# Chunked attention and a routed mixture of experts on one core: ranking candidates for a table of three slots, and new places for the picking, the evictions and the splits

## The chip, the cores and the metric

The kernel runs on one core of a Trainium2 chip. The metric is the device time of one execution in microseconds; before the change it is 582.98 us, the median of three runs (580.61 to 583.99).

## The reference

Attention runs inside chunks of 64 tokens (8 batches, 8 heads, 576 tokens, head size 64). Its output is the input of a layer of 8 experts, of which each token takes the one with the largest logit.

```python
scores = scale * np.matmul(q_c, k_c.transpose(0, 1, 2, 4, 3))
scores = scores - np.max(scores, axis=-1, keepdims=True)
attn = np.exp(scores)
attn = attn / (np.sum(attn, axis=-1, keepdims=True) + 1e-09)
out = np.matmul(attn, v_c)
...
logits = x @ w_gate + modality_bias[modality_id]
e_idx = np.argmax(logits, axis=1)
...
for e in range(E):
    mask = e_idx == e
    h = np.maximum(x[mask] @ w1[e], 0.0)
    out[mask] = gate_w[mask, None] * (h @ w2[e])
```

x has 4608 rows of 512 values, the hidden size is 1024, and gate_w is the softmax probability of the chosen expert.

## The kernel before

**Attention in rounds.** A round r works on two blocks of 128 tokens. `scores(r)` makes 64 small matmuls into the PSUM tile `sb`, then DVE takes the row maximum (`mx`, L236) and the difference to it (`ex`, L237). `exps` takes the exponent on ACT and adds halves on POOL (`sr`, L245). `transposes` turns `ex` into the two banks `ts`, ACT copies them to `at`; `values` multiplies with v into the same two banks; `evict` copies them to `xt` on ACT (L281). `rows(t)` multiplies a block with the identity and the gate weights at once (L290), into one of the two bank pairs `pairs`; DVE scales the result (`xr`, L292) for the copy `xd` in DRAM, and `parts` copies the gate part to `lp` on ACT (L300). Rounds 0 to 7 run alone, in the loop at L947; the other ten are merged into the first slots by `merge`, one piece at each `tick`. Each engine takes its instructions in the order in which the program emits them (`manual_schedule`), so the order of the calls is the order of the queues.

**Choosing slots.** Tokens are sorted by expert into slots of 384 rows (11 of them, then two of 256). Slot 0 is picked from the first 8 blocks (`route0`): POOL makes the logits (`logits`), DVE finds each token's expert (`gmx` to `oh`, L342 to L347), PE ranks tokens by matmuls with a triangle and with ones (L350, L352), DVE picks the fullest expert and makes a list of rows (`top` to `vm`, L354 to L377), eight small matmuls add it up (L382), and `tk` holds it (L385). `gather` then fetches the rows from `xd` with three indirect DMAs of POOL (L685). Slots 1 to 3 come from a table made after 16 blocks by `early_table`: three times it finds the expert with the most rows left, takes up to 384 of them and subtracts. The other slots come from `slot_table`. `route(g)` ranks the groups of blocks behind the first; it needs a spare bank for its two matmuls (L458, L459), and a running sum over the blocks, `scan`, which DVE makes before them. `blank` and `locate` read rows of the tables into registers of SP, which holds up SP's later DMAs, the fetches of weights among them.

**Experts in steps.** A slot has eight steps f, numbered over all slots g = 8 s + f. `first` makes 12 matmuls (L800) with a tick in their middle, ACT and DVE make `hh` and `hl` of the result; `second` of the step before makes 9 for three tiles (L816). Numbers are split into a high and a low part. For weights this is `wsplit`: a cast `wh` on ACT (L759) and a difference `wl` on DVE (L763), from `raw`, which `fetch` loads two steps at a time. In slot 0, `LEAD` says which splits follow which step; later it is step g + 4, with six buffers. For the rows of slots 0 and 1 PE transposes `xg` (`split`, L726); for later slots it goes by way of DRAM (`stash`, `place`, `turn`, `part`).

**What sets the order.** `PLAN` names, for a round and one of three places in it, calls that are made there. `PREP` does so for the ends of steps. Jobs such as `route` and `early_table` are generators: each `advance` (twice or three times a step, and at each `hook` of a round) runs one piece, up to its next yield.

Of the kernel before, what the change touches and what calls it, by code (L numbers as in the profile page):

```python
# [87 lines left out]
C_END = C_TH3 + NTT + 1  # L88
# [3 lines left out]
def attention_moe(ctx: ExitStack, tc: tile.TileContext, qkv, mod, cst, bias, wcat, wfst, void, out):  # L92
# [60 lines left out]
    th3 = cs[:, C_TH3:C_TH3 + NTT + 1]  # L153

# [71 lines left out]
    def scores(r, bank):  # L226
        b = qks.pop(r)
        sp = bank.rearrange("p u (h k) -> p u h k", h=H)
        for h in range(H):
            for u in range(2):  # L230
                us = slice(u * 64, u * 64 + 64)
                for c in range(2):
                    PE.matmul(sp[c * 64:c * 64 + 64, u, h, :], b[us, 0, h, c], b[us, 1, h, c], start=True, stop=True)  # L233
        ex = exs[r] = ak.tile([P, H, 2, 64], F32, name="ex", bufs=2)
# [94 lines left out]

    def route0():  # L330
# [37 lines left out]
        yield  # L368
# [9 lines left out]
                        val.unsqueeze(2).to_broadcast([P, n, NTT, 2]), ALU.mult)  # L378
        yield
# [25 lines left out]
    def route(g):  # L405
# [7 lines left out]
        early, last = g < NLEV, g == len(GROUPS) - 1  # L413
        l0 = lps[g % 2][:, 0:n]
# [28 lines left out]
        while d < n:  # L443
# [14 lines left out]
        PE.matmul(rp[:, 0, 0:n], ub, oh, start=True, stop=True)  # L458
        PE.matmul(rp[:, 1, 0:n + 1], ones, scan[i][:, off:off + n + 1], start=True, stop=True)  # L459
        V.tensor_tensor(base[g + 1], base[g], rp[:, 1, n], ALU.add)  # L460
        ra = tl("ra")
        V.tensor_tensor(ra, rp[:, 0, 0:n], base[g].unsqueeze(1).to_broadcast([P, n, E]), ALU.add)
# [329 lines left out]
    def first(x, w, f, n):  # L792
# [4 lines left out]
        for k in range(NK):  # L797
# [4 lines left out]
            if k == 1:  # L802
                tick()
# [271 lines left out]
```

## Time and profile before

| | before |
|---|---|
| median of three runs | 582.98 us |
| the profiled execution | 583.71 us |
| its span | 581.9 us |
| PE busy | 532.6 us (92%) |
| DVE busy | 359.9 us (62%) |
| ACT busy | 242.2 us (42%) |
| POOL busy | 165.6 us (28%) |
| mean granted clock of PE | 0.971 |
| HBM read and written | 101.91 MB, 27.83 MB |

Times within the profile are counted from the start of the span. A busy PE says little by itself: where the whole span is 92% busy, the idle 8% and the stretches of low clock are the parts to look at, and a table by windows shows where they lie. In a row of the timeline the brackets hold the idle time of the engine before it and what ended it. Rounds 0 to 7 take the first 66 us, the merged rounds reach to about 200 us, and the steps of the later slots fill the rest.

### The profile page before, as it was taken

The numbers are of one execution on the slowest core, as the hardware profiler recorded it, in microseconds if no ns is written. First come the engines' busy times: TensorE is split into PE (matmuls) and PEld (weight loads), VectorE is DVE, ScalarE is ACT, GpSimd is POOL, SyncE is SP. The second block draws the span as 40 slices with busy tenths as digits, with TensorE's granted clock in tenths as the row PEclk, the third lists the DMA queues.
The fourth block names the chain that finished last, engine by engine and source line by source line (L and its number), as shares of the span: only waits on it lengthen the run. The fifth ranks groups of instructions, "written<-read, shape, count | busy, mean of one in ns | idle before, by whom it ended". The sixth has DMA issues, their size and how long they took to land.

```text
span 581.9 us, 12230 instructions
## 1 busy us (share of the span) xinstructions
PE 532.6 (92%) x4930; PEld 476.1 (82%) x4931; DVE 359.9 (62%) x613; ACT 242.2 (42%) x401; POOL 165.6 (28%) x185
## 2 busy tenths in 40 slices
PE   6886587799878999999999999999999999999993
PEld 3776477688767988898899989889989898998982
DVE  4568557867577596865646556564655656456741
ACT  3444424354535433343434444434343434335530
POOL 3331426523343576042050212204041220402001
PEclk9899978899989999999999999999999999999997
DMA  8999954488758426958596574748667673756400
GB/s 339 402 325 315 355 214 151 149 304 294 271 190 283 150 64 203 336 206 310 175 288 220 161 275 151 274 155 304 202 207 229 170 257 128 244 180 210 175 34 26
DMA packets 48626, 129.83 MB, mean 223 GB/s; under 512 B 7100, under 2 KB 23852, under 8 KB 39600
## 3 DMA queue, kind: packets, MB, share of 16 engines
q1 hardware_dynamic: 36592, 100.35, 51.1%
q0 software_dynamic: 7072, 19.18, 9.2%
q10 hardware_dynamic: 4896, 9.44, 4.4%
q8 instruction: 40, 0.66, 0.5%
q14 instruction: 26, 0.21, 0.1%
HBM read 101.91 MB, written 27.83 MB: 223 GB/s over the span
## 4 chain that ended last, share of the span: by engine, by line
PE 66%; issue 14%; DVE 8%; DMA 7%; POOL 2%; ACT 1%; SPq 0%; POOLq 0%; ACTq 0%; DVEq 0%
PE y L800 24%; PE sb L816 17%; PE t L816 9%; PE t L800 4%; PE y L290 3%; DMA xg<-xd,tk 3%; DMA qk<-in_qkv 2%; PE y L273 2%; DVE wl L763 2%; PE y L233 2%; PE y L258 2%; DVE mx L236 1%; DVE ex L237 1%; PE sb L233 1%; POOL out L831 1%
## 5 line engine op out<-in xcount | busy, mean ns | idle before, releaser
L763 DVE TENSOR_TENSOR wl<-raw,wh 128x1024 fp32r<-128x1024 f32 x104 | 127.2, 1225 | 38.3 <-ACT wh L759 38.2
L800 PE MATMUL y<-xh,wh 128*128 128x384 f32 (+1 forms) x368 | 120.5, 328 | 0.0
L800 PE MATMUL y<-xl,wh 128*128 128x384 f32 (+1 forms) x368 | 120.4, 327 | 0.0
L800 PE MATMUL y<-xh,wl 128*128 128x384 f32 (+1 forms) x368 | 120.0, 326 | 0.0
L806 ACT ACTIVATE hh<-y 128x384 fp32r<-128x384 f32 (+1 forms) x92 | 43.6, 474 | 182.8 <-PE y L800 182.6
L807 DVE SCALAR_TENSOR_TENSOR hl<-y,hh 128x384 fp32r<-128x384 f32 (+1 forms) x92 | 49.1, 534 | 105.6 <-ACT hh L806 105.5
L759 ACT CAST wh<-raw 128x1024 fp32r<-128x1024 f32 x104 | 108.2, 1043 | 6.3 <-DMA raw<-in_wcat 6.1
L831 POOL DMA_INDIRECT out<-yo,tk x37 | 38.0, 1027 | 239.8 <-DVE yo L830 210.7
L816 PE MATMUL sb<-wh,hl 128*128 128x512 f32 x208 | 83.3, 400 | 1.3 <-DVE hl L807 1.3
L816 PE MATMUL sb<-wh,hh 128*128 128x512 f32 x208 | 83.3, 400 | 0.0
L816 PE MATMUL sb<-wl,hh 128*128 128x512 f32 x208 | 82.5, 397 | 0.0
L800 PEld LDWEIGHTS y<-xh,wh 128*128 128x128 f32 x368 | 69.1, 188 | 3.6
L800 PEld LDWEIGHTS y<-xl,wh 128*128 128x128 f32 x368 | 69.2, 188 | 3.4
L800 PEld LDWEIGHTS y<-xh,wl 128*128 128x128 f32 x368 | 69.2, 188 | 0.0
L816 PEld LDWEIGHTS sb<-wh,hl 128*128 128x128 f32 x208 | 39.3, 189 | 11.1 <-DVE hl L807 1.7
L685 POOL DMA_INDIRECT xg<-xd,tk x37 | 42.8, 1156 | 16.6 <-issue 10.7
L480 POOL DMA_INDIRECT tab<-tg,pi x36 | 38.8, 1078 | 23.0 <-issue 12.2
L816 PEld LDWEIGHTS sb<-wh,hh 128*128 128x128 f32 x208 | 39.2, 188 | 5.9
L816 PEld LDWEIGHTS sb<-wl,hh 128*128 128x128 f32 x208 | 39.2, 189 | 5.6
L245 POOL TENSOR_TENSOR sr<-ex 128x512 f32<-128x512 f32 x18 | 24.3, 1351 | 67.9 <-ACT ex L243 67.9
L290 PE MATMUL y<-cs,xt 128*128 128x144 f32 x288 | 41.5, 293 | 1.7 <-DVE e_tab L364 1.3
L290 PEld LDWEIGHTS y<-cs,xt 128*128 128x128 f32 x288 | 38.6, 194 | 3.2 <-DVE base L361 1.4
(225 smaller groups left out, 714.9 us busy)
## 6 DMA issues: line engine op xcount, KB each, us to landing
raw<-in_wcat SPq DMA_DIRECT2D x44, 1024.0 KB, 6.2
qk<-in_qkv SPq DMA_DIRECT2D x18, 1024.0 KB, 7.5
v<-in_qkv SPq DMA_DIRECT2D x18, 512.0 KB, 4.7
xd<-xr ACTq DMA_DIRECT2D x18, 512.0 KB, 7.3
raw<-in_wfst SPq DMA_DIRECT2D x8, 1024.0 KB, 9.5
xs<-xg SPq DMA_DIRECT2D x9, 768.0 KB, 7.7
xq<-xs SPq DMA_DIRECT2D x36, 192.0 KB, 3.8
xs<-xg SPq DMA_DIRECT2D x2, 512.0 KB, 6.6
```

The source lines that it names most:

```text
L233: PE.matmul(sp[c * 64:c * 64 + 64, u, h, :], b[us, 0, h, c], b[us, 1, h, c], start=True, stop=True)
L245: G.tensor_tensor(sring[r % 2][:, :, :, 0:32], exu[:, :, :, 0:32], exu[:, :, :, 32:64], ALU.add)
L290: PE.matmul(fp[:, p, 0:GWC], xt[:, p, :], gw[:, p, :], start=True, stop=True)
L480: w = G.indirect_dma_start(tab, bass.IndirectOffsetOnAxis(ap=pi[:, j:j + 1], axis=0), tg[:, j, :], None, bounds_check=E * CAP - 1, oob_is_ ...
L685: G.indirect_dma_start(xg[:, t, :], None, xd[0:n, :], bass.IndirectOffsetOnAxis(ap=tk[:, t:t + 1], axis=0), bounds_check=n - 1, oob_is_err ...
L759: A.copy(hi, raw)
L763: (G if pool else V).tensor_tensor(lo, raw, hi.bitcast(F32), ALU.subtract)
L800: PE.matmul(hp, a[:, ks], b[:, k, 0:n], start=(m == 0), stop=(m == 3 * NK - 1))
L806: A.activation(hh[:, 0:n], hp, AF.Relu)
L807: V.scalar_tensor_tensor(hl[:, 0:n], hp, 0.0, hh.bitcast(F32)[:, 0:n], ALU.max, ALU.subtract)
L816: PE.matmul(y, a[:, tsl], b[:, DM:2 * DM], start=(f == 0 and i == 0), stop=(f == NF - 1 and i == 2))
L831: w = G.indirect_dma_start(out, bass.IndirectOffsetOnAxis(ap=tk[:, t:t + 1], axis=0), yo, None, bounds_check=N - 1, oob_is_err=False)
```

## The change

- `early_table` no longer takes one maximum after the other. Each expert gives three candidates (its rows left, less 0, 384 and 768), 24 in all. All pairs are compared in one operation (576 results in bf16), a sum over them gives each candidate's rank, and the three with ranks 0, 1 and 2 are selected together with their expert, row and quantity.
- `scores` keeps its matmuls only; `differences` holds mx and ex. In a round the hook stands between the two, and a second one behind them: the picking of slot 0 is emitted there one round earlier, with both of its DVE parts in one piece. Gather, fetch and split calls of `PLAN` move with it.
- `evict(r)` is emitted behind the second `rows` of its own round, ahead of `parts`, with four buffers for `xt`.
- For group 1 the ranking is made by nine matmuls as in `route0`, without the scan. For groups 2 and 3 one more yield stands before the ranking.
- `AHEAD = 3`: weights are split three steps ahead, with five buffers, and slot 0 has at most one split after each of its steps 0 to 2.
- The two splits of slot 1's rows are made inside `first` of steps 6 and 7 (`AMID`); blank, locate, gather and settle of `PREP` move up by a step.

```diff
-    5: {2: ["fetch 0"]},
-    6: {1: ["gather 0"]},
+    5: {3: ["fetch 0"]},
+    6: {0: ["gather 0"], 3: ["hi 0"]},
...
-LEAD = ((2,), (3, 4), (5,), (6,), (7, 8), (9,), (10,), (11,))
+AHEAD = 3
+AMID = {6: "split 1 0", 7: "split 1 2"}
...
-    0: {2: ["choose"], 3: ["blank 1"], 4: ["settle", "locate 1"],
-        5: ["gather 1", "head"], 6: ["locate 2", "locate 3", "split 1 0"], 7: ["split 1 2", "gather 2"]},
+    0: {2: ["choose", "blank 1"], 3: ["settle", "locate 1"],
+        4: ["gather 1", "head"], 5: ["locate 2", "locate 3"], 7: ["gather 2"]},
...
+    def differences(r, bank):
+        sp = bank.rearrange("p u (h k) -> p u h k", h=H)
         ex = exs[r] = ak.tile([P, H, 2, 64], F32, name="ex", bufs=2)
...
+    def rank_tiles(rp, oh, n):
+        PE.matmul(rp, ub, oh, start=True, stop=False)
+        for t in range(n):
+            PE.matmul(rp[:, t + 1:], ones, oh[:, t:t + 1].to_broadcast([P, n - t, E]), start=False, stop=(t == n - 1))
...
         V.tensor_tensor(col, col, rank, ALU.add)
-        yield
         ge = wk.tile([P, n, NTT + 1], F32, name="ge0", bufs=1)
...
-        while d < n:
+        while d < n and not early:
...
+        if not early:
+            yield
         yield "rp"
...
+        V.scalar_tensor_tensor(cand, be(left), 32.0, offs, ALU.mult, ALU.add)
+        cand = cand.rearrange("p e j -> p (e j)")
+        more = t3("more", [C, C], BF16)
+        V.tensor_tensor(more, cand.unsqueeze(1).to_broadcast([P, C, C]), cand.unsqueeze(2).to_broadcast([P, C, C]), ALU.is_gt)
+        yield
+        rank = t3("rank3", [C])
+        V.reduce_sum(rank, more, axis=AX.X)
+        yield
...
+        V.tensor_tensor(ohs, rank.unsqueeze(1).to_broadcast([P, ne, C]), sid[:, 0:ne].unsqueeze(2).to_broadcast([P, ne, C]), ALU.is_equal)
+        sel = t3("sel", [3, ne, C])
...
+        V.reduce_sum(rf, sel, axis=AX.X)
+        yield
...
-    WB = 6
+    WB = 5
...
             if k == 1:
                 tick()
+                if g in AMID:
+                    call(AMID[g])
...
-            if s == 0:
-                for k in LEAD[f]:
+            if s == 0 and f < 4:
+                for k in ((2,), (3,), (4,), (5, 6))[f]:
                     wsplit(k)
-            elif g + 4 < end:
-                wsplit(g + 4)
+            elif g + AHEAD < end:
+                wsplit(g + AHEAD)
...
     for r in range(NPURE):
-        if r:
-            evict(r - 1)
         scores(r + 1, sb)
         hook(r, 0)
+        differences(r + 1, sb)
+        hook(r, 1)
         transposes(r, ts)
         if r:
             rows(2 * r - 2, pairs[0])
         exps(r + 1)
         values(r, ts)
-        hook(r, 1)
+        hook(r, 2)
         if r:
             rows(2 * r - 1, pairs[1])
+        evict(r)
+        if r:
             parts(r - 1)
             put(r - 1)
+        hook(r, 3)
         sums(r)
-        hook(r, 2)
```

How this moves instructions is shown at three places. On DVE, in rounds 5 and 6, the list of slot 0 (`ge` to `vm`, then `idf` and `tk`) stood in two parts; `mx` and `ex` are the maximum and difference of round 6's scores. Before:

```order
L249 TENSOR_REDUCE sm<-sr_145 128x16
L250 RECIPROCAL ris<-sm 128x16
L370 TENSOR_TENSOR ge_912<-col,cs 128x32
L372 SCALAR_TENSOR_TENSOR col<-ge_912,col 128x8
L373 SCALAR_TENSOR_TENSOR col<-ge_912,col 128x8
L374 TENSOR_TENSOR ge_912<-ge_912 128x8x3
L375 TENSOR_TENSOR xg<-xq,col 128x1024
L377 TENSOR_TENSOR vm<-ge_912,val 128x48
L236 TENSOR_REDUCE mx<-sb 128x16
L237 TENSOR_TENSOR ex<-sb,mx 128x2x8x64
L384 TENSOR_SCALAR idf<-y_99 128x3
L385 TENSOR_TENSOR tk_170<-idf,y_99 128x3
```

The same part of DVE's order now (line numbers of the changed kernel):

```order
L382 TENSOR_TENSOR ge_846<-col,cs 128x32
L384 SCALAR_TENSOR_TENSOR col<-ge_846,col 128x8
L385 SCALAR_TENSOR_TENSOR col<-ge_846,col 128x8
L386 TENSOR_TENSOR ge_846<-ge_846 128x8x3
L387 TENSOR_TENSOR xg<-xq,col 128x1024
L389 TENSOR_TENSOR vm<-ge_846,val 128x48
L302 TENSOR_TENSOR xr<-y_98,ris 128x4x4x32
L302 TENSOR_TENSOR xr<-y_99,ris 128x4x4x32
L397 TENSOR_SCALAR idf<-y_99 128x3
L398 TENSOR_TENSOR tk_169<-idf,y_99 128x3
L259 TENSOR_REDUCE sm<-sr_145 128x16
L260 RECIPROCAL ris<-sm 128x16
```

The list is now made ahead of round 5's two xr, and `tk` stands ahead of the next mx and ex. On POOL, the gather of slot 0 (`xg<-xd`) stood behind two `sr` that follow the last logits; before:

```order
L320 TENSOR_TENSOR lg_148<-lg_148,mb 128x16
L245 TENSOR_TENSOR sr_144<-ex 128x16x32
L245 TENSOR_TENSOR sr_145<-ex 128x16x32
L685 DMA xg<-xd,tk_170 128x512 x3
L245 TENSOR_TENSOR sr_144<-ex 128x16x32
```

And now:

```order
L330 TENSOR_TENSOR lg_148<-lg_148,mb 128x16
L255 TENSOR_TENSOR sr_144<-ex 128x16x32
L717 DMA xg<-xd,tk_169 128x512 x3
L255 TENSOR_TENSOR sr_145<-ex 128x16x32
L255 TENSOR_TENSOR sr_144<-ex 128x16x32
```

The gather has one `sr` less ahead of it. On PE, at the end of step 6 and the start of step 7 of slot 0, the split of slot 1's rows (`xg`) stood between the `rows` (`xt`) of two blocks and the next `first` (`t<-xh`, `t<-xl`); `y<-cs,ex` are transposes of attention. Before:

```order
L290 MATMUL y_98<-cs,xt 128x144 x4
L290 MATMUL y_99<-cs,xt 128x144 x4
L726 MATMUL y_98<-cs,xg 128x128 x6
L800 MATMUL t_102<-xh_165,wh_155 128x384
L800 MATMUL t_102<-xl_166,wh_155 128x384
L800 MATMUL t_102<-xh_165,wl_156 128x384
...
L258 MATMUL y_99<-cs,ex 128x128 x8
```

And now:

```order
L300 MATMUL y_99<-cs,xt 128x144 x4
L300 MATMUL y_98<-cs,xt 128x144 x4
L833 MATMUL t_102<-xh_164,wh_158 128x384
L833 MATMUL t_102<-xl_165,wh_158 128x384
L833 MATMUL t_102<-xh_164,wl_159 128x384
...
L268 MATMUL y_99<-cs,ex 128x128 x8
L758 MATMUL y_98<-cs,xg 128x128 x6
```

The split follows the transposes inside `first`, and the bank that it takes is no longer the one of the first `rows`.

More of the change, by code (lines that the diff above doesn't have):

```diff
@@ L153, in attention_moe @@
     th3 = cs[:, C_TH3:C_TH3 + NTT + 1]
+    offs, steps3, eid3 = (cs[:, c:c + 3 * E].rearrange("p (e j) -> p e j", j=3) for c in (C_OFF, C_JS, C_E3))
+    far = cs[:, C_FAR:C_FAR + 3]
     warm = cp.tile([P, 512], BF16, name="warm")
@@ L349, in route0 @@
         rp = pairs[1][:, 0, 0:(n + 1) * E].rearrange("p (t e) -> p t e", e=E)
-        PE.matmul(rp, ub, oh0, start=True, stop=False)
-        for t in range(n):
-            PE.matmul(rp[:, t + 1:], ones, oh0[:, t:t + 1].to_broadcast([P, n - t, E]), start=False, stop=(t == n - 1))
+        rank_tiles(rp, oh0, n)
         most, vt, ft = (wk.tile([P, m], F32, name=f"top{i}", bufs=1) for i, m in enumerate((1, E, 1)))
@@ L413, in route @@
         early, last = g < NLEV, g == len(GROUPS) - 1
+        if early:
+            oh0 = cp.tile([P, n + 1, E], BF16, name=f"oh{g}")
+            G.memset(oh0[:, n], 0.0)
         l0 = lps[g % 2][:, 0:n]
@@ L434, in route @@
         off = OFF
-        oh = tl("oh", BF16)
+        oh = oh0[:, 0:n] if early else tl("oh", BF16)
         V.tensor_tensor(oh, va, bc(fm, n), ALU.is_equal)
-        V.tensor_copy(scan[0][:, off + 1:off + 1 + n], oh)
+        if not early:
+            V.tensor_copy(scan[0][:, off + 1:off + 1 + n], oh)
         yield
@@ L455, in route @@
         V.reciprocal(tg.bitcast(F32)[:, :, 1], gs)
+        if not early:
+            yield
         yield "rp"
         rp = rpbank[0].rearrange("p (a b c) -> p a b c", a=2, b=32)
[L458 to L460 removed]
         ra = tl("ra")
[L462 to L463 removed]
+        if early:
+            rank_tiles(rp[:, 0, 0:n + 1], oh0, n)
+            V.tensor_tensor(base[g + 1], base[g], rp[:, 0, n], ALU.add)
+            V.tensor_tensor(ra, rp[:, 0, 0:n], base[g].unsqueeze(1).to_broadcast([P, n, E]), ALU.add)
+        else:
+            PE.matmul(rp[:, 0, 0:n], ub, oh, start=True, stop=True)
+            PE.matmul(rp[:, 1, 0:n + 1], ones, scan[i][:, off:off + n + 1], start=True, stop=True)
+            V.tensor_tensor(base[g + 1], base[g], rp[:, 1, n], ALU.add)
+            V.tensor_tensor(ra, rp[:, 0, 0:n], base[g].unsqueeze(1).to_broadcast([P, n, E]), ALU.add)
+            V.tensor_tensor(ra, ra, rp[:, 1, 0:n], ALU.add)
         V.tensor_tensor(ra, ra, oh, ALU.mult)
@@ new lines, in early_table @@
+        V.tensor_tensor(sel, ohs.unsqueeze(1).to_broadcast([P, 3, ne, C]),
+                        qty.rearrange("p q e j -> p q (e j)").unsqueeze(2).to_broadcast([P, 3, ne, C]), ALU.mult)
+        rf = t3("ef", [3, ne])
+        V.reduce_sum(rf, sel, axis=AX.X)
+        yield
+        end, full = t3("eend", [ne]), t3("efull", [ne])
+        V.tensor_tensor(end, rf[:, 1], rf[:, 2], ALU.add)
+        V.scalar_tensor_tensor(full, rf[:, 2], float(SLOT), far, ALU.is_ge, ALU.mult)
+        V.tensor_tensor(rf[:, 2], end, full, ALU.max)
@@ L849, in slot @@
             place(s)
-            for f in range(4):
+            for f in range(AHEAD):
                 wsplit(s * NF + f)
@@ L988, in merge @@
             if r + 1 < NR:
-                scores(r + 1, pair())
+                bank = pair()
+                scores(r + 1, bank)
+                differences(r + 1, bank)
                 later(1, exps, r + 1)
```

82 lines of the change are left out of this document (38 added, 44 removed).

## The prediction

> **What bounds the kernel now.** I read the span by windows first, to see where TensorE (PE) is full and where it isn't. The columns are PE, weight loads, DVE, ACT and POOL busy time, then granted clock, DMA share and GB/s.
>
> ```profile
> 72.00:80.00 8.00, 6.03 (x24) 5.74 (x25) 3.12 (x4) 1.81 (x3) 0.00 (x0) 0.50 0.87 362
> 96.00:100.00 4.00, 3.13 (x15) 3.03 (x15) 3.17 (x10) 0.42 (x2) 2.09 (x2) 0.67 0.46 169
> 168.00:172.00 4.00, 3.96 (x15) 3.24 (x16) 2.45 (x7) 1.20 (x3) 2.04 (x2) 0.63 0.47 148
> 300.00:340.00 40.00, 40.00 (x200) 35.98 (x199) 22.00 (x30) 16.61 (x25) 10.04 (x10) 1.00 0.72 235
> ```
>
> From about 235 us on, as in the last row, PE has no idle time and the full clock; 200 matmuls in 40 us at 21 a step (12 in first, 9 in second) make a step of 4.2 us. Nothing can be won there but by fewer matmuls, and the change removes none. So the gain has to come from the time before 235 us: from idle PE, and from the clock of 0.50 to 0.67 that the other rows show behind idle stretches. The waits of PE say whose they are: in the attention rounds (20 to 66 us), then at the gather of slot 0 with its DMA's time to landing, then in the merged part (90 to 240 us).
>
> ```profile
> PE t L258 <- ACT xt L281: 3.0, 4, 0.8
> PE y L382 <- DVE vm L377: 2.6, 1, 2.6
> ```
>
> ```profile
> PE sb L726 <- DMA xg<-xd,tk: 7.6, 3, 4.7
> ```
>
> ```profile
> DMA to landing us min/median/max: 11.4/11.6/11.8
> ```
>
> ```profile
> PE y L258 <- ACT lp L300: 4.4, 2, 4.0
> PE y L726 <- ACT lp L300: 3.2, 2, 2.9
> PE y L458 <- ACT lp L300: 2.3, 1, 2.3
> PE sb L816 <- DVE hl L807: 1.3, 1, 1.3
> PE y L726 <- DMA xg<-xd,tk: 1.1, 1, 1.1
> PE y L459 <- DVE scan L447: 1.0, 1, 1.0
> ```
>
> The largest single wait is the 7.6 us for the rows of slot 0, and the half clock of the first row follows it. Almost every line of these is touched by the change.
>
> **The change part by part.** First the rounds and the gather. These are the rows of before that time them, on PE, then DVE, then POOL.
>
> ```profile
> 42.90 1.16 PE L233 MATMUL sb<-qk 64*64 64x64 f32 x64
> ...
> 78.38 0.69 PE L800 MATMUL t<-xh,wh 128*128 128x384 f32 x1
> ```
>
> ```profile
> 45.78 1.22 DVE L237 TENSOR_TENSOR ex<-sb,mx 128x1024 f32<-128x1024 f32 x1
> 46.92 0.21 DVE L342 TENSOR_REDUCE gmx<-lg 128x8 f32<-128x64 f32 x1
> ...
> 47.93 0.22 DVE L347 TENSOR_TENSOR oh<-va,fm 128x64 bf16<-128x64 f32 x1
> ...
> 48.70 0.17 DVE L354 TENSOR_REDUCE top<-y 128x1 f32<-128x8 f32 x1
> ...
> 51.16 0.69 DVE L292 TENSOR_TENSOR xr<-y,ris 128x512 f32<-128x512 f32 x1 [0.88 <-PE y L290]
> 51.76 0.69 DVE L249 TENSOR_REDUCE sm<-sr 128x16 f32<-128x528 f32 x1
> ...
> 52.66 0.13 DVE L370 TENSOR_TENSOR ge<-col,cs 128x32 f32<-128x32 f32 x1
> ...
> 53.33 1.22 DVE L375 TENSOR_TENSOR xg<-xq,col 128x1024 bf16<-128x1024 f32 x1
> 54.46 0.20 DVE L377 TENSOR_TENSOR vm<-ge,val 128x48 bf16<-128x48 f32 x1
> ```
>
> ```profile
> 45.60 0.22 POOL L320 TENSOR_TENSOR lg<-lg,mb 128x16 f32<-128x16 f32 x1
> ...
> 59.73 1.24 POOL L685 DMA_INDIRECT xg<-xd,tk  x1 [0.17 <-DMA qk<-in_qkv]
> ...
> 62.58 1.00 POOL L685 DMA_INDIRECT xg<-xd,tk  x1 [0.30 <-issue]
> ```
>
> Evictions: evict(r) now stands ahead of parts in ACT's queue, so the transposes of the next round find their banks empty. The four waits of 3.0 us go; two lie before round 5, which therefore starts 1.5 us earlier, at 41.4 instead of 42.90. The evictions fall where ACT has nothing else to do, and the lp copies that they now precede wait for DVE's xr anyway.
>
> The picking in round 5: scores run 1.16 us, to 42.6. POOL ended its last logits op 2.9 us after the round's start (45.82 against 42.90); as much now gives 44.3. The five ops gmx to oh took 1.23 us (46.92 to 48.15), so oh is there at 45.5. This is an added wait: the ranking matmuls stand ahead of transposes(5), so PE idles from 42.6 to 45.5, 2.9 us, with transposes, values and rows queued behind. Then DVE does mx and ex (2.4 at 1.2 each, by the row of ex), top to col (1.6, from 48.70 until xr's idle time of 0.88 begins at 50.28), ge to vm (2.0, 52.66 to 54.66) and two xr (1.3): 45.5 + 7.3 = 52.8. The list's eight small matmuls wait for the last xr and the lp copy behind it, then idf and tk follow: 1.0 us by the neighbouring small rows, tk at 53.8. Round 6 then starts at 53.4 and round 7 at 58.9, at 5.5 us of matmuls a round, so that attention ends near 64.5; the time that PE loses in round 5 is about what the evictions had saved.
>
> What is won is the gather. In before it was queued on POOL behind the sr of round 6 and issued from 59.73 to 62.58. Now it stands ahead of that sr, right behind tk: 53.9 to 56.7, 5.9 us earlier. Its landing decides. With its own 11.6 us of before the third tile lands at 68.3; with no DMA traffic in its way it could be far shorter, and then the next limit is DVE, where lo 0, lo 1 and two xl end at about 69. I take 9.5 us (66.2), nearer its own row than half of it, since round 5 now lasts 12 us for the same bytes and the engines have less queued. First matmuls come 3.4 us after the third landing (3.9 in before, at half clock): 69.6 against 78.38. **Term 1: -8.8 us**, from -6.7 (landing 11.6) to -9.4 (DVE).
>
> Now the merged part, slot 0 and the start of slots 1 and 2. Two rows bound the stretch of DVE that the old table holds before xr, and one carries the price of a weight split.
>
> ```profile
> 106.53 0.16 DVE L498 TENSOR_TENSOR left<-base,cs 128x8 f32<-128x8 f32 x1
> ...
> 112.10 1.28 DVE L292 TENSOR_TENSOR xr<-y,ris 128x512 f32<-128x512 f32 x2
> ```
>
> ```profile
> L763 DVE TENSOR_TENSOR wl<-raw,wh 128x1024 fp32r<-128x1024 f32 x104 | 127.2, 1225 | 38.3 <-ACT wh L759 38.2
> ```
>
> Fewer splits in step 1: one wl of 1.225 us stands ahead of xr instead of two, so the 2.3 us wait at L458 becomes 1.1. The nine ranking matmuls in place of two cost at most 0.55 us (48.15 to 48.70, where route0's nine ran), I take 0.3. The clock was 0.67 for 4 us behind the wait, 1.3 us lost; with half the wait I count 0.9 of it back. Together -1.8 (0 to -2.3).
>
> The table: 5.57 us from 106.53 to xr, less a wl of 1.22, are 26 ops in 4.35, 0.167 each. Now 12 stand ahead of xr: eight small ones (1.4), two of 576 elements, which lie between 528 at 0.69 and 1024 at 1.22, so 0.75 each, and two of 216, about 0.37 each: 3.65. PE's wait of 4.0 becomes 3.3: -0.7 (+0.3 if the reads of broadcast operands cost more, -1.1 if the sum over bf16 runs at double rate). No clock comes back.
>
> Splits of slot 1 inside first, and gather 1 one step earlier: the 1.1 us for DMA goes, because POOL now comes to the gather one step, and one sr, earlier. Of the waits behind lp (3.2) about 0.7 stays, since the next transposes need the same bank one second-call later. New is that scores wait for the split's xl behind xh, 0 to 1 us, I take 0.5. Of the clock of 0.63 behind it (1.5 lost in 4 us) I count 0.8 back. Together -3.9 (-1 to -5).
>
> The extra yield for groups 2 and 3: the scan is finished when its matmul comes, -1.0. One weight fetch now passes SP ahead of the eight loads of stop, so a cast that waits for it on ACT no longer holds back hh and with it hl at L816: -1.3 (0 to -1.3). SP's next fetch still waits behind them, but AHEAD = 3 asks for its weights one step later, 4.2 us.
>
> **Term 2: -1.8 - 0.7 - 3.9 - 1.0 - 1.3 = -8.7 us** (-3 to -11).
>
> AHEAD = 3 and five weight buffers I cost at nothing in the full part: a split issued behind first(g) has three steps less one first, 10.5 us, until first(g+3), and needs about 1.0 on ACT and 1.2 on DVE, which is busy 22 of 40 us. That slack is the cover; the second rival says what it costs if it's gone.
>
> The profiled execution took 583.71 us, 1.8 above its span of 581.9 and 0.7 above the median of 582.98. 583.71 - 8.8 - 8.7 = 566.2.
>
> One rule speaks about these clocks. The rows show 0.67 in the window behind a wait of 2.3 us and 0.63 behind one of 2.9. The Trainium skill, page "TensorE: Matmul & The Clock Gate", Part 1, has the clock halved only after an idle window of about 3.4 us; the trace disagrees, as both waits were shorter. By that rule the 1.7 us of clock that I count back would stay away, and the sum would be 567.9.
>
> **The rivals.** First: the gather is issued earlier but lands hardly earlier, because the DMA engines are full anyway (share 0.87 in the first window, 362 GB/s) and the same bytes must move before slot 0. For it: its own 11.6 us. Against: three gathers are 0.8 MB, and qk and v are loaded three rounds ahead, so others can wait. Landing at 72 instead of 74.4 leaves -2.4 and term 2: 583.7 - 2.4 - 8.7 = 572.6. Chance 0.17. The Trainium skill, page "DMA: Bandwidth & Descriptors", section "Queues, rings and completion order", has each DMA engine alternate between queues that have work, so a gather wouldn't stand behind SP's backlog; by that the end at DVE's 69 would hold, 565.6, and no row here shows it.
>
> Second, slower: the weight lead becomes the bound. If a landing is so late that the split of g+3 isn't done by first(g+3), PE waits in each step, as it did once at L816 for 1.3 us. It decides where landing and queues eat the 10.5 - 2.2 = 8.3 us of slack. For it: ACT and DVE are in order, and hh and hl share them. Against: raw is asked for as early as before and used a step later. At 0.25 us in each of 92 steps it is +23: 566.2 + 23 = 589. Chance 0.09.
>
> Third, no change: the 2.9 us that PE now waits for oh, and as much for the list, halve the clock in rounds 5 to 7 (1.3 to 1.5 us each as behind the other waits), attention ends after 70, the gather's gain is gone, and behind the early splits PE waits for xl instead of lp, so that term 2 keeps only its last 2.3: 583.7 - 0 - 2.3 = 581.4. Against: the 2.6 us wait at L382 wasn't followed by a slow round. Chance 0.08.
>
> **How the numbers follow.** The forecast has 0.66, by its bounds 562 to 572 (both terms rarely at one end). The first rival lies at 572.6 with term 2's spread. Range 560 to 575.5, which leaves out the second and third rival, 0.17. Half a per cent, 2.9 us, is about what a measurement of this kernel tells from no change: faster 0.83, same 0.08, slower 0.09. The likeliest is 566.2.
>
> **What would show it.** In the profile of after: no wait of t L268 for xt; a wait of PE near 3 us for oh in round 5; the three gathers issued 53 to 57 us in; first(0) near 69.6 and a wait for xg below 2.5 us; the wait for lp ahead of step 3 near 3.3 us; no PE wait at a split of slot 1 over 1 us; PE full from about 220 us at 4.2 us a step. It is wrong if the gathers land after 70, if the windows behind 220 us show idle PE, or if the span's end moves by less than first(0) does.

## The result and the profile after

| | before | after |
|---|---|---|
| median | 583.43 us (580.61 to 583.99, 4 runs) | 568.31 us (564.73 to 569.24, 4 runs) |
| ratio | | 0.9739, 95% interval 0.9685 to 0.9793 |
| the profiled execution, its span | 583.71, 581.9 us | 567.62, 565.8 us |
| mean granted clock of PE | 0.971 | 0.986 |

The changed kernel is faster by 15 us; 566.2 was forecast, with a range of 560 to 575.5. The median of before has one run more here than the 582.98 that the forecast started from. The ratios of e1 to e4 and e9 to e12 below leave out the profiled execution and single executions that were over 1.5% slower than the fastest of the same kernel. Line numbers are now those of the changed kernel (scores L240, transposes L268, values L283, rows L300, ranking L341, list L395, gather L717, first L833, second L851). First the windows of PE, with the columns of the prediction's first fence.

```profile
36.00:40.00 4.00, 1.81 (x10) 1.71 (x10) 1.50 (x3) 0.37 (x1) 1.89 (x5) 0.79 0.86 285
...
48.00:52.00 4.00, 3.46 (x23) 3.46 (x24) 3.82 (x13) 1.64 (x3) 0.00 (x0) 0.57 0.81 312
...
72.00:80.00 8.00, 6.75 (x47) 6.09 (x45) 7.05 (x11) 3.64 (x7) 2.67 (x3) 1.00 1.02 419
...
100.00:104.00 4.00, 1.38 (x9) 1.05 (x7) 3.90 (x11) 0.21 (x1) 2.60 (x2) 1.00 0.16 66
```

Where slot 0 starts (72 to 80 us) the clock was 0.50 and is now 1.00. The low clock now stands in the rounds, at 0.79 and 0.57. The waits of PE, from 20 to 66 us and then from 82 to 232 us:

```profile
PE y L341 <- DVE oh L362: 3.1, 1, 3.1
PE sb L240 <- issue: 2.7, 1, 2.7
PE y L395 <- ACT lp L310: 2.3, 1, 2.3
PE t L283 <- issue: 2.1, 2, 1.9
```

```profile
PE y L268 <- ACT lp L310: 4.3, 3, 2.6
PE y L240 <- issue: 2.4, 1, 2.4
...
PE y L341 <- ACT lp L310: 1.2, 1, 1.2
```

The four waits for xt are gone, the wait for oh is there, and of the rows waiting for the gather (7.6 us before) 0.9 is left. The waits at the splits of slot 1, for scan and for hl behind 230 us, are gone too. PE's timeline shows what the rounds made of it (first the end of round 4's scores before the change, then the changed kernel).

```profile
38.43 0.27 PE L233 MATMUL sb<-qk 64*64 64x64 f32 x2 [1.31 <-issue]
```

```profile
34.30 1.15 PE L240 MATMUL sb<-qk 64*64 64x64 f32 x62
38.19 0.30 PE L240 MATMUL sb<-qk 64*64 64x64 f32 x2 [2.73 <-issue]
38.42 1.97 PE L268 MATMUL t<-cs,ex 128*128 128x128 f32 x8
...
44.28 1.16 PE L240 MATMUL sb<-qk 64*64 64x64 f32 x64
48.54 0.24 PE L341 MATMUL y<-oh,ub 128*128 128x72 bf16 x1 [3.10 <-DVE oh L362]
...
48.90 1.95 PE L268 MATMUL t<-cs,ex 128*128 128x128 f32 x8
...
57.29 1.16 PE L240 MATMUL sb<-qk 64*64 64x64 f32 x64
...
69.09 1.25 PE L300 MATMUL y<-cs,xt 128*128 128x144 f32 x8
...
71.47 0.66 PE L758 MATMUL sb<-cs,xg 128*128 128x128 f32 x4 [0.91 <-DMA xg<-xd,tk]
...
73.50 0.43 PE L833 MATMUL t<-xh,wh 128*128 128x384 f32 x1
```

Round 4 starts 1.66 us earlier than before (34.30 against 35.96), but its scores stop for 2.73 us two matmuls before their end (1.31 at the same place before), and the transposes behind run at half clock, 1.97 us for eight instead of 1.09. So round 5 starts later than before, at 44.28. Attention ends at 70.3, and the first expert step begins at 73.50: 4.9 us of the 16.1 between the spans are won there, 11.2 behind it. The steps can be followed by the start of DVE's hl in each (one in every first; read from DVE's timelines; "again" is a later run of the changed kernel):

| hl of step | 0 | 1 | 2 | 3 | 4 | 6 | 7 | slot 1: 0 | 1 | 3 |
|---|---|---|---|---|---|---|---|---|---|---|
| before | 83.2 | 89.0 | 102.3 | 117.5 | 127.4 | 146.5 | 158.5 | 179.2 | 186.5 | 202.7 |
| after | 77.7 | 83.6 | 94.4 | 109.1 | 117.8 | 140.4 | 150.6 | 166.3 | 172.3 | 188.7 |
| again | 77.2 | 83.0 | 93.9 | 109.3 | 118.0 | 139.5 | 149.7 | 165.4 | 171.4 | 187.8 |
| won (after) | 5.4 | 5.4 | 7.9 | 8.4 | 9.5 | 6.1 | 7.9 | 12.9 | 14.2 | 14.0 |

### The profile page after: what moved, and what is told of

It is laid out like the page before. It is cut to its first block, busy times and chain, and to the rows that moved or that the text cites. A ratio compares the mean times of both kernels' runs of the same rounds, so it can differ in the third digit from the quotient of the medians.

```text
span 565.8 us, 12228 instructions
## 1 busy us (share of the span) xinstructions
PE 526.5 (93%) x4938; PEld 473.0 (84%) x4938; DVE 357.6 (63%) x590; ACT 241.8 (43%) x401; POOL 166.6 (29%) x186
## 4 chain that ended last, share of the span: by engine, by line
PE 60%; issue 15%; DVE 4%; POOL 3%; ACT 1%; POOLq 0%; ACTq 0%; DVEq 0%
PE y L833 26%; PE sb L851 18%; PE t L851 9%; PE t L833 2%; PE y L300 2%; POOL out L866 1%; PE y L240 1%; DVE wl L795 1%; PE y L268 1%; POOL tab L504 1%; DVE mx L246 1%; PE y L283 1%; DVE xr L302 0%; ACT at L271 0%; DVE xl L761 0%
## 5 line engine op out<-in xcount | busy, mean ns | idle before, releaser
L833 PE MATMUL y<-xh,wh 128*128 128x384 f32 (+1 forms) x368 | 120.7, 328 | 0.0
L833 PE MATMUL y<-xh,wl 128*128 128x384 f32 (+1 forms) x368 | 120.7, 328 | 0.0
L833 PE MATMUL y<-xl,wh 128*128 128x384 f32 (+1 forms) x368 | 120.1, 326 | 0.0
L851 PE MATMUL sb<-wh,hh 128*128 128x512 f32 x208 | 82.7, 398 | 0.0
L851 PE MATMUL sb<-wh,hl 128*128 128x512 f32 x208 | 82.4, 396 | 0.0
L851 PE MATMUL sb<-wl,hh 128*128 128x512 f32 x208 | 82.0, 394 | 0.0
L833 PEld LDWEIGHTS y<-xl,wh 128*128 128x128 f32 x368 | 69.3, 188 | 3.6
L833 PEld LDWEIGHTS y<-xh,wh 128*128 128x128 f32 x368 | 69.4, 189 | 3.4
L833 PEld LDWEIGHTS y<-xh,wl 128*128 128x128 f32 x368 | 69.2, 188 | 0.0
L717 POOL DMA_INDIRECT xg<-xd,tk x37 | 41.9, 1131 | 17.4 <-issue 7.3
L851 PEld LDWEIGHTS sb<-wh,hl 128*128 128x128 f32 x208 | 39.0, 188 | 9.0
L504 POOL DMA_INDIRECT tab<-tg,pi x36 | 40.6, 1127 | 19.1 <-issue 11.0
L300 PE MATMUL y<-cs,xt 128*128 128x144 f32 x288 | 43.2, 300 | 1.3 <-DVE ex L247 1.3
L851 PEld LDWEIGHTS sb<-wh,hh 128*128 128x128 f32 x208 | 39.1, 188 | 5.7
L851 PEld LDWEIGHTS sb<-wl,hh 128*128 128x128 f32 x208 | 39.1, 188 | 4.8
L300 PEld LDWEIGHTS y<-cs,xt 128*128 128x128 f32 x288 | 40.1, 200 | 3.0 <-DVE ex L247 1.7
```

Of the source, the lines that this page charges most:

```text
L300: PE.matmul(fp[:, p, 0:GWC], xt[:, p, :], gw[:, p, :], start=True, stop=True)
L504: w = G.indirect_dma_start(tab, bass.IndirectOffsetOnAxis(ap=pi[:, j:j + 1], axis=0), tg[:, j, :], None, bounds_check=E * CAP - 1, oob_is_ ...
L717: G.indirect_dma_start(xg[:, t, :], None, xd[0:n, :], bass.IndirectOffsetOnAxis(ap=tk[:, t:t + 1], axis=0), bounds_check=n - 1, oob_is_err ...
L833: PE.matmul(hp, a[:, ks], b[:, k, 0:n], start=(m == 0), stop=(m == 3 * NK - 1))
L851: PE.matmul(y, a[:, tsl], b[:, DM:2 * DM], start=(f == 0 and i == 0), stop=(f == NF - 1 and i == 2))
```

## The experiments

The theory at this point: the parts in the merged stretch (splits of weights in step 1, table, splits of rows, yields) won 11 us, each by a PE wait that it takes away and the clock behind it; the rounds won only 5, since PE's waits there lowered the clock. The rivals were that one part makes the gain (the table or the evictions), and that slot 0's start doesn't matter. Runs that share a chip share the runs of the kernel before, whose median is given: 581.3 us (first four runs), 603.8 (next four), 582.0 (e9 to e11) and 604.2 (e12). The chips of e5 to e8 and of e12 take 20 us longer for the kernel before (last section). The changed kernel itself didn't run on these two: by time their variants are compared with the kernel before, and with the changed kernel only by distances from the start of round 5 in the traces.

**Undoing one part at a time.** The rounds as before (e1):

```diff
-    6: {0: ["gather 0"], 3: ["hi 0"]},
+    6: {1: ["gather 0"]},
...
         scores(r + 1, sb)
+        differences(r + 1, sb)
         hook(r, 0)
```

> The changed kernel with rounds 0 to 7 as they were before: eviction at the top of the next round, picking, gather and fetch at their old places; table, splits, lead and yields stay changed. Theory (the rounds gave 4.9 us, by the start of the first expert step, and these come through to the end): first expert step back near 78.4 us, time 568.3 + 4.9 = about 573, with half clock behind the 7.6 us wait for the rows of slot 0 up to 575. Rival (slot 0's start doesn't matter, since what follows waits for DVE and ACT anyway): within 1 us of 568.3.

```profile
73.13 0.33 PE L758 MATMUL sb<-cs,xg 128*128 128x128 f32 x1 [3.29 <-DMA xg<-xd,tk]
75.32 1.11 PE L758 MATMUL sb<-cs,xg 128*128 128x128 f32 x4 [1.85 <-DMA xg<-xd,tk]
...
79.26 0.69 PE L833 MATMUL t<-xh,wh 128*128 128x384 f32 x1
```

570.5 us, ratio 0.9792 (0.9742 to 0.9843). The wait for the gather is back with 5.1 us, the first step at 79.26, and step 7's hl is at 158.5, 7.9 us behind the changed kernel's. The trace bears the theory out, but it is that of the longest of the four executions (575.2 us; the others took 568.6, 568.8 and 572.1). By the time (0.5 points of ratio, overlapping intervals) the run stands between the theory's 573 and the rival's 568.

The table as before (e2), PE ahead of step 3:

```diff
-        more = t3("more", [C, C], BF16)
...
+        for i in range(ne):
...
+            V.reduce_max(mx, left, axis=AX.X)
```

> The changed kernel with the old early_table, one maximum after the other; all else stays changed. Theory (the table gave 0.7 us plus the clock behind the wait): PE's wait for lp ahead of step 3's transposes 3.3 to 4.0 us instead of 2.6, time +0.7 us if the clock stays full, up to +2.5 us with half clock behind the wait: 569 to 571. Rival (the table, the only part named first in the change, is what makes the gain): +6 us or more, 574 and above.

```profile
102.31 1.97 PE L268 MATMUL y<-cs,ex 128*128 128x128 f32 x8 [3.68 <-ACT lp L310]
```

570.5 us, ratio 0.9799 (0.9741 to 0.9856). The wait is 3.68 us instead of 2.65, with half clock behind it, as the theory said; the rival's 574 is above the interval.

Slot 1's splits behind their steps again (e3):

```diff
-AMID = {6: "split 1 0", 7: "split 1 2"}
+AMID = {}
```

> The changed kernel with slot 1's two splits behind steps 6 and 7 instead of inside their first, and blank, locate and gather of slot 0's steps at their old places; all else stays changed. Theory (the splits gave 3.9 us): waits for lp and for the gather's rows at the two splits come back, 3 to 4 us together, time 571 to 573. Rival (these waits only pass to the next stage, which waits for DVE): within 1 us of 568.3.

```profile
PE y L758 <- ACT lp L310: 3.2, 2, 2.9
PE y L758 <- DMA xg<-xd,tk: 1.6, 2, 1.3
```

573.8 us, ratio 0.9795 (0.9724 to 0.9865). The four executions lie between 567.7 and 576.5 us, and the ratio rests on two of them (567.65 and 572.32), so the time says little. In the trace the 4.8 us of waits are back, and from hl of step 4 to that of step 1 of slot 1 it takes 60.7 us (119.9 to 180.6) instead of 54.4: 6.3 us, more than the theory's 3 to 4, although the issue stall in that stretch is shorter (0.80 us instead of 2.43). This is the largest of the parts behind the start of slot 0.

Two weight splits behind step 1 (e4):

```diff
-                for k in ((2,), (3,), (4,), (5, 6))[f]:
+                for k in ((2,), (3, 4), (5,), (6,))[f]:
```

> The changed kernel with two weight splits behind step 1 of slot 0, as before, instead of one, and one instead of two behind step 3; all else stays changed. Theory (a split's wl of 1.2 us stands on DVE ahead of xr): PE's wait for lp ahead of the ranking matmuls 2.3 instead of 1.2 us, time +1.1 us, with clock lost behind it up to +2: 569.4 to 570.3; the wait ahead of step 3 doesn't change. Rival (the wait at step 3 takes up what step 1 loses, since both are held by the same DVE queue): the wait at step 3 shorter by 1 us, time within 0.5 us of 568.3.

```profile
PE y L268 <- ACT lp L310: 3.6, 2, 2.8
PE y L341 <- ACT lp L310: 2.3, 1, 2.3
```

570.3 us, ratio 0.9817 (0.9768 to 0.9867). The wait at L341 is 2.3 us, as expected; the one ahead of step 3 is no shorter, so the rival falls. The intervals of e1 to e4 all overlap that of the changed kernel: it is the waits in the traces, not the times, that tell the parts apart.

The extra yield (e11):

```diff
-        if not early:
-            yield
         yield "rp"
```

> The changed kernel without the extra yield ahead of the ranking of groups 2 and 3. Theory (the yield gives DVE time to finish the running sum): a PE wait of 1.0 us for scan comes back near 170 to 180 us, time +1.0 us (under what a repetition moves). Rival (nothing, since DVE is ahead there by now): no PE wait over 0.3 us at the ranking matmuls.

```profile
169.01 0.21 PE L482 MATMUL y<-scan,ones 128*128 128x104 bf16 x1 [1.04 <-DVE scan L464]
...
178.94 0.40 PE L849 MATMUL t<-wh,hl 128*128 128x512 f32 x1 [2.38 <-issue]
```

570.6 us, ratio 0.9803 (0.9763 to 0.9844). The wait for scan is back with 1.04 us; the profile shows no effect of the yield that would explain the rest of the 3.2 us to the changed kernel on that chip (567.4). The profiled execution has an issue stall of 2.38 us there.

The evictions alone, in the kernel before (e5):

```diff
-            evict(r - 1)
...
             rows(2 * r - 1, pairs[1])
+        evict(r)
```

> The kernel before, with only the evictions moved to their new place (with two buffers for xt, as before, which makes the second copy wait for the rows matmuls just ahead of it). Theory (the four PE waits for xt were 3.0 us, but the gather of slot 0 waits for the picking and not for the rounds): the waits of the transposes for xt go, slot 0's first matmul 1 to 3 us earlier, time 579 to 582 beside 583. Rival (the evictions are the main part of the change): 575 or less.

602.4 us, ratio 0.9976 (0.9925 to 1.0028). No transposes wait for xt any more, and the time is hardly moved, so the evictions aren't the main part. But its first expert step is at 73.22, as early as the changed kernel's, and no row is waited for, although the gather stood at its old place and was issued later than in the kernel before (61.2 to 64.0 us): here the third tile must have landed within about 6.5 us, not 11.6. No trace of the kernel before was taken on that chip, and no run moves the picking without the evictions, so how the 4.9 us at the start of slot 0 divide between evictions and picking stays open.

**What sets the start of slot 0.** Warm matmuls while PE waits for oh (e6):

```diff
+        if r == 5:
+            busy(12)
         hook(r, 1)
```

> The changed kernel with 12 extra warm matmuls (128x512 bf16, 0.2 us each) on PE in round 5, while it waits for oh; their result isn't used. Theory (the half clock behind this wait comes from PE being idle): the wait for oh under 1 us, the eight transposes behind it 1.1 us instead of 1.95, clock 1.00 from 48 to 52 us; but the chain on DVE up to tk doesn't change, so the gather and the first expert step move by less than 1 us, and the time by less than 0.5%. Rival (the half clock comes from something else, such as the stretch of code loading ahead of it): the transposes stay at 1.9 us. Second rival (PE's clock in rounds 5 and 6 sets the gather): first expert step 2 us earlier.

```profile
46.04 0.19 PE L341 MATMUL y<-oh,ub 128*128 128x72 bf16 x1 [0.35 <-DVE oh L362]
...
46.28 1.07 PE L268 MATMUL t<-cs,ex 128*128 128x128 f32 x8
...
54.50 0.35 PE L395 MATMUL y<-vm,xg 128*128 128x6 bf16 x8 [3.83 <-ACT lp L310]
54.79 1.99 PE L240 MATMUL sb<-qk 64*64 64x64 f32 x64
```

Idle PE is what lowers the clock: with the warm matmuls the transposes take 1.07 us. But PE then waits 3.83 us for the list instead of 2.3, and half clock follows there. Round 6 starts 13.0 us behind round 5 (41.77), as without them, and the first expert step 29.6 us behind it (29.2 without), so the second rival falls; ratio 0.9886 (0.9761 to 1.0012). DVE sets the length of round 5. So I moved the list and the gather on DVE and POOL (e7):

```diff
+    5: {2: ["gather 0"], 3: ["fetch 0"]},
...
-        yield
-        got = pairs[1][:, 0, 0:2 * NTT].rearrange("p (t c) -> p t c", c=2)
+        got = sb[:, 0, 0:2 * NTT].rearrange("p (t c) -> p t c", c=2)
```

> The changed kernel with the eight list matmuls of slot 0 in the bank sb right behind values of round 5 instead of behind the lp copies, idf and tk ahead of round 5's second xr, and the gather emitted there, ahead of sm and ris. Theory (the gather is held by DVE's chain from oh to tk, 9.4 us, then by ris, 1.0 us): oh to tk about 8.3 us, gather issued behind tk at once, so 2.2 us earlier against the start of round 5 (12.2 instead of 14.4 us behind it); landing 9.4 us unchanged; first expert step 1.5 to 2.2 us earlier against the start of round 5 (27.0 to 27.7 instead of 29.2 us behind it). Rival (the landing is set by the DMA queues, which are full until 70 us): the landing becomes longer by as much as the issue is earlier, first expert step at 29 us behind round 5. Time by the theory 0.3% below the changed kernel.

```profile
42.44 1.16 PE L240 MATMUL sb<-qk 64*64 64x64 f32 x64
...
53.63 0.35 PE L394 MATMUL sb<-vm,xg 128*128 128x6 bf16 x8 [1.89 <-DVE vm L389]
...
72.21 0.43 PE L832 MATMUL t<-xh,wh 128*128 128x384 f32 x1
```

```profile
55.34 1.24 POOL L716 DMA_INDIRECT xg<-xd,tk  x1 [3.46 <-DVE tk L397]
```

The gather is issued 12.9 us behind round 5 (14.4 in the changed kernel), PE waits for no row of it, and yet the first step comes 29.8 us behind round 5, not earlier than the 29.2 of the changed kernel. The theory's 27.0 to 27.7 is missed, and the rival's mechanism isn't it either: the end of attention (69.5) binds, and PE waits 1.9 us for vm. On this chip that was so already: e6, with its gather issued 14.4 us behind round 5, waits for no row either, so e7 doesn't show what an earlier gather is worth where rows are waited for. It is 0.9 us from tk to the gather here too, so ris never held the gather. Ratio 0.9968 (0.9914 to 1.0023).

Both together (e8):

```diff
+            busy(12)
...
+            busy(10)
         hook(r, 2)
```

> As the run with the early gather, and 12 warm matmuls ahead of the ranking and 10 ahead of the list matmuls in round 5. Theory (idle PE halves the clock behind the wait, DVE sets the gather): clock 1.00 through rounds 5 and 6, start of round 6 within 13 us of round 5; gather as in the run without warm matmuls, within 0.5 us; time within 0.3% of that run. Rival (clock in rounds 5 to 7 decides): attention ends and the first expert step starts 2 us earlier than without them.

Rounds 5 and 6 start 12.6 us apart (43.65 and 56.27), the clock is 1.00 from 44 to 57 us, and the gather is issued 13.0 us behind round 5, all as the theory had it. But an issue stall of 3.64 us in round 7 covers what follows, and the first step is at 78.59, so the rival can't be judged. The median of 596.2 us is 0.7% below e7's 600.3, not within the theory's 0.3. Ratio 0.9876 (0.9772 to 0.9979).

So the next run lets both come earlier, the end of attention and the gather. With the whole picking ahead of mx and ex, and transposes and rows ahead of the ranking (e10, beside the changed kernel again, e9):

```diff
+        if r != 5:
             differences(r + 1, sb)
             hook(r, 1)
         transposes(r, ts)
         if r:
             rows(2 * r - 2, pairs[0])
+        if r == 5:
+            hook(r, 1)
...
         hook(r, 2)
+        if r == 5:
+            differences(r + 1, sb)
+            exps(r + 1)
```

> The changed kernel itself, run again beside the next two on the same chip, to see what a repetition moves. Theory (stretches in which PE's instructions arrive late, and the half clock behind short waits, differ from run to run, while the order of the work stays): the rounds end and slot 0 starts within 3 us of the 70.3 and 73.5 us of the first profile, the distance from round 5 to the first expert step stays at 29 us within 0.5, and the time stays 2 to 3% below the kernel before on a chip like the first.

> The changed kernel with round 5 in another order: transposes and the first rows ahead of the ranking matmuls on PE, and on DVE the whole picking (top to vm, idf, tk) ahead of mx and ex of round 6; the gather is emitted behind tk. Theory (the first expert step waits for two things of nearly the same length, the end of attention and the landing, so that both must come earlier): tk 9.1 us behind the start of round 5 instead of 13.4, gather issued at 10 instead of 14.4, round 6 at 11.5 instead of 13.0, first expert step 27 to 28 instead of 29 us behind the start of round 5; time 1 to 2 us below the changed kernel. Rival (the end of attention alone decides and the waits in round 5 only change their place): first expert step at 29 us, same time. Second rival (a PE wait of 2.5 us for vm brings half clock in round 5 or 6): first expert step later than 29 us.

PE, then DVE, then the landing of the run that picks first:

```profile
43.79 1.16 PE L240 MATMUL sb<-qk 64*64 64x64 f32 x64
...
52.25 0.36 PE L394 MATMUL y<-vm,xg 128*128 128x6 bf16 x8 [2.71 <-DVE vm L389]
...
55.45 1.99 PE L240 MATMUL sb<-qk 64*64 64x64 f32 x64
...
70.79 0.43 PE L832 MATMUL t<-xh,wh 128*128 128x384 f32 x1
```

```profile
50.36 0.17 DVE L384 SCALAR_TENSOR_TENSOR col<-ge,col 128x8 f32<-128x8 f32 x1
...
52.84 0.16 DVE L397 TENSOR_TENSOR tk<-idf,y 128x3 int32<-128x3 f32 x1
```

```profile
DMA to landing us min/median/max: 6.0/6.5/7.4
```

The theory's distances behind round 5 hold: tk at 9.2, round 6 at 11.7, first step at 27.0 (expected 9.1, 11.5, 27 to 28). The changed kernel again has its first step 31.2 us behind round 5 (42.10 to 73.30), which misses the 29 that I expected of it: PE waited 2.4 us for the gather's rows there (landing 10.1 us), and the clock was 0.89 from 68 to 84 us. Its rounds end at 66.8, 3.5 us earlier than in the first profile, which misses the 3 us too. Side by side, in us behind the start of round 5:

| | attention ends | gather issued | PE waits for its rows | first step |
|---|---|---|---|---|
| changed kernel | 26.1 | 14.4 | 0.9 | 29.2 |
| changed kernel again (e9) | 24.7 | 14.4 | 2.4 | 31.2 |
| gather early (e7) | 27.1 | 12.9 | 0 | 29.8 |
| picking first (e10) | 24.6 | 10.1 | 0 | 27.0 |

In e9 attention ended as early as in e10, and the rows held the first step up; in e7 it was the other way round. Only e10, with both early, has an early first step. Part of that is the landing, 7.4 us at most instead of 9.4 and 10.1; what sets it isn't settled. Times: 567.43 us for the repetition, 0.9744 (0.9708 to 0.9780), and 566.82 for the picking first, 0.9709 (0.9662 to 0.9756). It has the lowest ratio of all that ran, but the 0.6 us between the medians is less than either interval, so a gain in time over the changed kernel isn't shown. In its profile the 2.5 us won by the first step are gone at step 7's hl (149.8 against 149.7): PE waits 0.8 us for xl in the first step, and 1.3 went to a longer issue stall near 118 us (2.63 against 1.30).

**The issue stalls (e12).** In the changed kernel's profile they come at PE's matmuls 221, 349, 730 and 2004 (counted as the profile counts them), about multiples of 128 apart; the profile's page has an instruction queue (packets, MB, share of the DMA engines):

```profile
q8 instruction: 40, 0.66, 0.5%
```

With 64 more tiny matmuls ahead of everything else but the first scores:

```diff
     busy(BUSY)
+    for i in range(64):
+        PE.matmul(pairs[1][0:64, 1, 0:64], warm[0:64, 0:64], warm[0:64, 0:64], start=True, stop=True)
```

> The run that picks first, with 64 more tiny warm matmuls (64x64 bf16, result not used) at PE's idle 1.6 us ahead of the second scores, which moves all later code of PE by 64 matmuls. Theory (PE's late instructions are blocks of code that come by DMA: in every run the stalls lie 128 matmuls or a multiple apart, at matmul 221, 349, 730 and 2004 of the changed kernel, always where the 128 before them were mostly 64x64 ones that take 3 to 4 us, and the profile's instruction queue moved 40 packets of 16.5 KB): no stall over 0.5 us inside round 4's scores and at the merged scores near 118 us, since the blocks that end there now take over 4.5 us; a stall inside the scores or values of rounds 1 to 3 instead, where blocks of 3.1 to 3.4 us end; time 1 to 4 us below the run that picks first. Rival (the stalls belong to these instructions, by a wait that the profile doesn't show): they stay at the last matmuls of round 4's scores and near 118 us, same time.

```profile
20.52 1.83 PE L300 MATMUL y<-cs,xt 128*128 128x144 f32 x7 [2.29 <-issue]
...
41.82 0.56 PE L283 MATMUL t<-at,v 64*64 64x64 f32 x18 [0.62 <-issue]
```

The stalls left round 4's scores, where four runs on the other slower chip (e5 to e8) still have 1.1 to 2.2 us. They now stand in the rows of round 1 (I had said scores or values), again at matmul 349 with the 64 counted in, and in round 4's values at 858, about four times 128 further on. In e8, too, with 22 warm matmuls added, the stall of round 7 came at matmul 1239 as in the changed kernel, though other instructions stand there. The rival, a hidden wait of these instructions, falls. Near 118 us this chip has stalls of another kind (below), so that part and the time (594.5 us, ratio 0.9868, 0.9810 to 0.9925) decide nothing.

## Why the prediction was right, and where it was not

The forecast was 2.1 us below the median, and the direction came about in the way it gave: waits at named places taken away. But its two terms were off in opposite directions, by 3.9 and 2.5 us, so that the sum came this close is in part luck. One of its own signs of being wrong came true: the gathers landed after 70, at 71.0.

**Term 1 was -8.8 and measured -4.9.** The failing step, by size, is "round 5 ... therefore starts 1.5 us earlier, at 41.4". These rows of DVE and POOL, and the landing of the gather, carry the rest:

```profile
48.26 0.22 DVE L362 TENSOR_TENSOR oh<-va,fm 128x64 bf16<-128x64 f32 x1
...
52.59 1.26 DVE L384 SCALAR_TENSOR_TENSOR col<-ge,col 128x8 f32<-128x8 f32 x1
...
57.67 0.16 DVE L398 TENSOR_TENSOR tk<-idf,y 128x3 int32<-128x3 f32 x1
```

```profile
52.56 1.27 POOL L255 TENSOR_TENSOR sr<-ex 128x512 f32<-128x512 f32 x1 [5.36 <-ACT ex L253]
58.72 1.24 POOL L717 DMA_INDIRECT xg<-xd,tk  x1 [4.89 <-DVE ris L260]
```

```profile
DMA to landing us min/median/max: 9.4/9.4/9.4
```

- Round 5 started at 44.28, 2.9 late, by the longer issue stall and the half clock in round 4. The evictions did their 1.5 (round 4 came 1.66 earlier). In other runs of the same rounds it started at 41.62 to 44.56, so the 41.4 was nearly within reach: this part of the miss changes from run to run. It isn't the whole miss either, since in e9 round 5 started at 42.10 and the first step still came at 73.30.
- oh came 4.2 us behind the round's start (4.1 forecast), the wait was 3.10 (2.9).
- From oh to tk it took 9.35 us instead of 8.3: the operation at L384 lasted 1.26 us beside POOL's sr, and 0.17 where POOL was idle (e10). The length comes back in every trace with the same order (9.25 to 9.35 us in e2, e3, e4, e6, e9 and e11), with the delay at L384 or at one of the two operations ahead of it (last section).
- The gather was issued 0.9 us behind tk, not 0.1; this comes back in every such trace too. Its landing, 9.4 us, was the 9.5 that I took.
- Behind the landing it took 2.5 us instead of 3.4 to the first step. 2.9 + 0.1 + 1.1 + 0.8 - 0.1 - 0.9 = 3.9, the whole miss.

Wrong in kind was "What is won is the gather" and "Its landing decides". Attention ended at 70.3 instead of 64.5, so that the rows were waited for by 0.9 us only: 2.9 us by the start of round 5, 1.0 by its length (13.0 instead of 12.0), 1.5 by round 6, which ran in part at half clock (7.0 instead of 5.5), and 0.5 by round 7. The forecast had charged the wait for oh to PE, but no half clock behind it or behind the wait for the list. The table of e10 shows that both ends have to be early. The third rival had named this (half clock in rounds 5 to 7, attention ending after 70) and was given 0.08; its mechanism came, its price didn't, since slot 0's start was no longer at half clock.

**Term 2 was -8.7 and measured -11.2.** By the table of hl:
- Step 0 won 0.5 by itself: its first matmuls are no longer at half clock. The forecast had nothing for it.
- Step 1 to 2 won 2.5 (forecast 1.8): the wait of 2.3 fell to 1.2 (forecast 1.1).
- The table and the clock behind it won 1.6 up to step 4 (0.7 forecast): the wait of 4.0 fell to 2.6, not to 3.3, and the clock stayed at 1.00. "No clock comes back" was wrong here. The sum over 576 values in bf16 took 0.74 us, no less than the 0.75 taken.
- From step 4 to 6, 3.4 were lost: the issue stall at L240 is 2.4 us (0.67 before, behind step 7), and PE now carries the first split inside step 6.
- From step 6 to step 0 of slot 1, 6.8 were won: the splits' waits of 4.3 went, and so did the stretch of low clock. The 0.7 that I left for lp is there (0.82 at the transposes at 159.09), the 0.5 for xl isn't. The forecast of 3.9 for the splits belongs beside both stretches together, 3.4, or 5.2 without the difference of the issue stalls; e3, which reaches one step further, gives 6.3.
- Then 1.3 for scan (1.0) and 1.9 to the end (1.3 for hl at L816).

AHEAD = 3 cost nothing in the full part, as forecast: from 232 to 400 us PE has no idle time, and the second rival didn't come.

```profile
232.00:400.00 168.00, 168.00 (x843) 1.00 0.73 228
```

The first rival (the gather lands hardly earlier, with full DMA engines) had the right place, 71.0 against 72, for another reason: not the landing was long, but the issue late.

## What to carry to other kernels

When two things end at nearly the same time, pricing one of them gives at most the distance to the other: look up both ends before counting a gain, and move both. A matmul that waits stands in the way of all behind it in PE's queue: it costs its wait, and perhaps half clock in what follows. Here independent matmuls put ahead of the ranking (e10) brought the wait for oh from 3.1 to 1.1 us. Parts of 1 to 4 us each can add up to 15 that no single comparison of times proves: read them from waits at named places.

## What the runs showed of the hardware

**The clock behind a wait of 2.6 to 2.8 us differs from run to run.** The same eight transposes ahead of step 3, behind nearly the same wait, in e11, e1 and the changed kernel:

```profile
103.56 1.97 PE L268 MATMUL y<-cs,ex 128*128 128x128 f32 x8 [2.65 <-ACT lp L310]
```

```profile
110.29 1.09 PE L268 MATMUL y<-cs,ex 128*128 128x128 f32 x8 [2.81 <-ACT lp L310]
```

```profile
104.02 1.09 PE L268 MATMUL y<-cs,ex 128*128 128x128 f32 x8 [2.65 <-ACT lp L310]
```

2.65 us brought half clock once and full clock once, 2.81 full clock. Of the nine traces with a wait of 2.64 to 2.84 us there, five show a low clock behind it (1.80 to 1.97 us for the eight) and four the full one. The wait of 3.1 us for oh in round 5 was followed by low clock in all seven traces that have it (1.79 to 1.95 us). The rule that I weighed (the Trainium skill, "TensorE: Matmul & The Clock Gate", Part 1: half clock after a window of about 3.4 us without work) agrees with the 3.68 us of e2, but 2.65, 2.73 and 3.10 us were enough in other places. The same part says that the window runs freely and so differs from run to run; that fits the difference between runs, while its length doesn't fit these waits.

**A small operation of DVE waited for POOL.** L384 (128x8) took 1.26 us from 52.59 on, beside POOL's sr of 1.27 us from 52.56 on, and 0.17 without it (e10). In e11 and e6 POOL's sr began at 51.75 and 49.61, earlier in the same list, and there L382 (51.82) and L380 (49.66) took 1.26 and 1.24 us instead of 0.19 and 0.17, while L384 took 0.17: the delay goes with POOL, not with the operation. The Trainium skill, "SBUF — State Buffer", section "SBUF: two separate sides", has DVE operations with two inputs in SBUF and POOL's share a pair of ports that whichever starts first holds for its whole instruction; the trace agrees, and this is the 1.1 us of the chain to tk that the forecast lacked.

**PE's instructions seem to come in blocks of 128 matmuls,** and where the block before is nearly all 64x64 matmuls (e12), the next is late by 0.6 to 2.7 us at the same count from run to run. In the changed kernel the instruction queue moved one packet within the stall of round 4 (35.5 to 38.2 us) and one within that near 120 us (119.2 to 121.8), which fits late code; that the packet is what PE waits for is inferred. The Trainium skill, "Runtime: NRT & Kernel Launch", section "Instruction fetch mechanics", states blocks of 256 instructions (a matmul and its weight load are two) and that loading them is mostly hidden; the spacing agrees, the hiding doesn't hold here.

**Two chips take 20 us more,** for the kernel before and for every variant that ran there. In e6, while POOL scatters the token table (80 to 87 us), PE gets its 64x64 matmuls four or five at a time, one such group in 0.72 us, and the DMA engines are nearly idle (share 0.17 from 80 to 88 us, 0.80 in the changed kernel on its chip). The 27 us between the spans of e6 and e9 all arise before 240 us; from there to 400 us PE has no idle time in e6 either. On those chips the variants of the changed kernel gain 1.1 to 1.3% (e6, e8, e12) or 0.3 (e7) over the kernel before, where the changed kernel gains 2.6 in both of its measurements elsewhere. Whether it would gain as much on the slower ones, and why they are slower, is not settled.
